# Column norms of the first mixture's weights taken in the middle chunks, and output tiles in another buffer ring, in a fused recurrence and two-mixture kernel

## The chip, the cores and the metric

The kernel runs on one NeuronCore of a Trainium2 chip. The metric is the device time of one execution in microseconds; of several executions the median is quoted. TensorE is called PE here (PEld its weight loads), VectorE DVE, ScalarE ACT, GpSimd POOL, and SyncE SP. The profile gives one execution in detail.

## The reference

Three stages follow each other. A recurrence over 768 time steps (batch 4, 8 heads, width 40), then two feed-forward mixtures over its 3072 x 320 output:

```python
for t in range(S):
    y[:, :, t] = einsum('bhd,bhde->bhe', rt, state)
    Sa = einsum('bhde,bhe->bhd', state, at)
    state = state * wt[:, :, None, :] - einsum('bhd,bhe->bhde', Sa, bt)
    state = state + einsum('bhd,bhe->bhde', vt, kt)
x = y.transpose(0, 2, 1, 3).reshape(B * S, H * D)
h = x @ w_in;   x = (h * cos(h)) @ w_out                          # first mixture, d_ff 2048
h = x @ w_in2;  out = (h * clip(h + 3, 0, 6) / 6) @ w_out2        # second mixture
```

## The kernel before, in words

The recurrence is cut into 12 chunks of 64 steps. A chunk of one batch entry is a unit (48 units), worked through by the functions `pA` to `cF`. The rows `xs` and `x1T` that a chunk leaves are the input of the first mixture for the chunk's 256 tokens, and what the first mixture leaves (`xs2`, transposed by DMA into `x2T` in `mT`) is the input of the second. `mA(m, c, j)` makes one block of the hidden layer of mixture m (m = 0 first, 1 second) for chunk c: 16 matmuls into a PSUM tile `h`, an ACT instruction into a tile `s`, a DVE multiplication in place, and two tiles of `ghl` (a half-precision value and its remainder). `mB(m, c, j)` multiplies such a block with `wout` into the PSUM tiles `acc0` and `acc1` (12 matmuls a block). Eight blocks make a chunk. After the eighth, `mB` copies each `acc` with ACT: for m = 0 into a buffer of the ring `xs2`, for m = 1 into an output tile `ob`, from which `mO` sends two DMAs to `out`.

Buffers are rings (`Rings`): `tile(tag)` hands out the buffers of a tag in turn, in the order in which the functions are called, and a buffer's next writer waits for its last reader. The rings `s` and `xs2` have two buffers each. Before the change `ob` is taken from the ring `s`, so the second `s` tile after it waits until the DMAs of `mO` have read the buffer.

All operations are first recorded by `Plan`, in the order of the numbers given to `at(...)`. That order sets the buffers and the dependences. Then `Plan.order` works out a start for every operation (an estimate of each duration, 50 passes forward and backward over all dependences) and writes the program in that order, engine by engine. So a change of one number in `at` can move rows anywhere in the program. Each engine executes its rows strictly in order, and all DMAs go through SP's queue.

`wcol(q)` (8 calls, line 802) takes the sums of squares of the columns of the first mixture's `win`: three ACT squares into one scratch stretch of `wstat` (called `junk`), two matmuls with a vector of ones after each, into the one PSUM buffer `p` that the units' function `pC` also uses, and a DVE reduction into `acc` (an SBUF table of range values, printed `acc_75` in the order, not the PSUM tiles). Its number is `T_WM + 44 + q`, that is 194 to 201, behind all units. `flags` (line 1164) is recorded last: it folds the table `acc` into one number `bad`. It reduces over the partitions by a DMA of 4 x 128 single elements to DRAM (`std`) and one back into a row, and every engine then loads `bad` and branches: the general version behind the branch is not run with these inputs.

Of the kernel before, what the change touches and what calls it, by code (L numbers as in the profile page):

```python
# [8 lines left out]
F32 = mybir.dt.float32  # L9
# [15 lines left out]
DM = H * D  # L25
# [17 lines left out]
T_P, D_P, T_I, D_I, T_C, D_C, T_M2, T_WM, LAG = 48.0, 2.0, 36.0, 4.0, 29.05, 2.1, 8, 150, 2  # L43
# [456 lines left out]
def kernel(  # L500
# [25 lines left out]
    p2 = Rings(big, 2)  # L526
# [73 lines left out]
    def at(t, fn, *a):  # L600
        heapq.heappush(ev, (t, seq[0], fn, a))
        seq[0] += 1

    def later(dt, fn, *a):
        at(now[0] + dt, fn, *a)
# [8 lines left out]
    def square(src, p0, p1_, n, nm, i, o=None):  # L614
        k = COL[nm][0] + i
        if o is None:
            o = junk[p0:p1_, 0:n]
        if len(src.shape) == 3:
            o = o.rearrange("p (a b) -> p a b", b=src.shape[2])
        nc.scalar.activation(out=o, in_=src, func=AF.Square, accum_out=acc[p0:p1_, k:k + 1])  # L620
# [502 lines left out]
    def mB(m, c, j, h=-1):  # L1123
        gg = G_t.pop((m, c, j, h))
        nf, w = (2, 256) if h < 0 else (4, 128)
        ts = (0, 1) if h < 0 else (h,)
        if j == 0:
            for t in ts:
                ACCS[m, c, t] = ps_a.tile([128, 512], F32, tag=f"acc{t}", name="acc")
        for k in range(nf):  # L1130
            f = nf * j + k
            for n, t in enumerate(ts):
                gs = slice(k * w + n * 128, k * w + (n + 1) * 128)
                for i, (gi, wi) in enumerate(((0, 0), (0, 1), (1, 0))):
                    nc.tensor.matmul(ACCS[m, c, t][:, 0:DM], gg[:, gi, gs], wout[m][:, wi, f, :],
                                     start=(f == 0 and i == 0), stop=(f == 15 and i == 2))
        if nf * (j + 1) < 16:
            return
        for t in ts:
            a = ACCS.pop((m, c, t))[:, 0:DM]  # L1140
            if m == 0:
                xs = p2.tile([128, 768], F16, tag="xs2", name="xs2")
                nc.scalar.activation(out=xs[:, 0:DM], in_=a, func=AF.Copy, scale=ISC)
                nc.vector.scalar_tensor_tensor(out=xs[:, 384:704], in0=a, scalar=ISC, in1=xs[:, 0:DM],
                                               op0=ALU.mult, op1=ALU.subtract)
                xv = xs.rearrange("p (x e) -> p x e", x=2)
                nc.either.tensor_copy(out=xv[:, :, 320:384], in_=xv[:, :, 256:320])
                square(xs[:, 0:DM], 0, 128, DM, "o1", 2 * c + t)
                at(16 * c + 15.8, mT, c, t, xs)
            else:  # L1150
                ob = p2.tile([128, DM], F32, tag="s", name="ob")
                nc.scalar.activation(out=ob, in_=a, func=AF.Copy, scale=ISC2)
                later(0.4, mO, c, t, ob)

# [224 lines left out]
    for c in range(NC):  # L1379
        for m in range(2):  # L1380
            base = 16 * c if m == 0 else 16 * (c + 1) + T_M2 if c < NC - 1 else 16 * NC
            for j in range(8):
                a = (m, c, j) if (m, c) not in HALVES else (m, c, j % 4, j // 4)
                at(base + j + 0.5, mA, *a)
                at(base + j + LAG + 0.9, mB, *a)
# [43 lines left out]
        for i in range(22):  # L1429
            at(T_WM + i + 22 * m, wmax, m, i)  # L1430
    for q in range(8):
        at(T_WM + 44 + q, wcol, q)
    while ev:
        now[0], _, fn, a = heapq.heappop(ev)
        nc.prio, nc.group = now[0], (fn.__name__, now[0]) + tuple(x for x in a if isinstance(x, int))
# [69 lines left out]
```

## Time and profile before

| | |
|---|---|
| median of 3 runs | 1151.99 us (1149.13 to 1154.26) |
| the profiled execution's own time | 1152.2 us |
| its span, first to last instruction | 1149.0 us |
| PE busy | 849.6 us (74%) |
| DVE busy | 987.8 us (86%) |
| ACT busy | 818.9 us (71%) |

The span has three stages. Up to about 350 us weights are loaded and decay products made, and the first chunks begin. From there to about 990 us units and both mixtures are interleaved. After that the mixtures of the last chunks remain, and the range number. A row of the chain view is time on the chain of work that ended last; a row of the timeline gives in brackets how long the engine sat idle and for whom.

### The profile page before, as it was taken

The page shows a single profiled execution, that of the slowest core. Times are in us where ns is not written, and L with a number is a line of the kernel's source. Part 1 is how long each engine was busy: PE and PEld are TensorE (multiplying, and loading weights), DVE is VectorE, ACT ScalarE, POOL GpSimd, SP SyncE. Part 2 cuts the span into 40 slices and gives each one's busy share as a digit, 9 for nine tenths or more (in the row PEclk, how much of TensorE's full clock was granted, in tenths as well). Part 3 has the DMA queues.
Part 4 walks back from the last instruction along what each step waited for, and adds up shares of the span by engine and source line. Part 5 has one row for each costly group of instructions (what it writes and reads, how often), then busy time and mean ns, then how long its engine had stood idle before and what let it go on. Part 6 is the DMA issues. An engine that isn't in the chain of part 4 may idle for free. (4 is left out here: it accounts for less than half of the span.)

```text
span 1149.0 us, 29397 instructions
## 1 busy us (share of the span) xinstructions
PE 849.6 (74%) x11378; PEld 686.3 (60%) x11378; DVE 987.8 (86%) x2359; ACT 818.9 (71%) x1720; POOL 37.6 (3%) x131
## 2 busy tenths in 40 slices
PE   0010123728887989899999788899889989999993
PEld 0000023626675767677877667687667768788872
DVE  7789999999899798798997888988989879998552
ACT  5775578999998797695876867868759756573241
POOL 3000000000000000000000000000000000000000
PEclk9999999957898999999999899899899999999997
DMA  6989878998987878768958768689786744521010
GB/s 213 269 188 274 176 175 167 236 210 180 211 169 148 161 132 141 132 111 166 162 96 167 129 120 160 119 155 149 126 165 122 135 95 74 108 42 34 2 26 16
DMA packets 476279, 162.62 MB, mean 142 GB/s; under 512 B 446405, under 2 KB 458737, under 8 KB 475746
## 3 DMA queue, kind: packets, MB, share of 16 engines
q1 hardware_dynamic: 475842, 159.99, 70.2%
q8 instruction: 91, 1.49, 0.5%
q10 hardware_dynamic: 288, 0.67, 0.2%
q14 instruction: 58, 0.48, 0.1%
HBM read 80.09 MB, written 25.61 MB: 92 GB/s over the span
## 5 line engine op out<-in xcount | busy, mean ns | idle before, releaser
L456 PE MATMUL acc<-wout,ghl 128*128 128x320 f16 x2304 | 362.8, 306 | 24.5 <-DVE ghl L456 17.4
L456 PEld LDWEIGHTS <-win 128*128 128x128 f16 x3328 | 310.8, 101 | 72.3 <-issue 31.4
L456 PEld LDWEIGHTS <-ghl 128*128 128x128 f16 x2304 | 218.6, 100 | 109.8 <-DVE ghl L456 22.8
L456 ACT ACTIVATE s<-h,cvec 128x512 f32<-128x512 f32 x192 | 130.5, 682 | 119.5 <-PE h L456 66.2
L456 PE MATMUL h<-x1T,win 128*128 128x256 f16 (+1 forms) x1664 | 190.4, 272 | 19.8 <-DVE s L456 19.2
L456 PE MATMUL h<-x2T,win 128*128 128x256 f16 (+1 forms) x1664 | 188.2, 269 | 7.1 <-DVE s L456 5.6
L456 DVE TENSOR_TENSOR ghl<-s,ghl 128x512 f16<-128x512 f32 x192 | 130.9, 683 | 5.4 <-ACT ghl L452 3.1
L456 PE MATMUL p<-ART,KBT 120*128 120x64 f16 x384 | 21.9, 206 | 115.6 <-DMA KBT<-KBs 81.0
L456 DVE TENSOR_TENSOR tmp<-Tt,Lt 128x126 f32<-128x126 f32 (+22 forms) x372 | 91.0, 245 | 8.7 <-DMA Lt<-Ls 6.4
L456 DVE SCALAR_TENSOR_TENSOR s<-h,s 128x512 f32<-128x512 f32 x96 | 65.6, 685 | 36.2 <-ACT s L456 35.4
L456 DVE TENSOR_TENSOR Tt<-Tt,tmp 128x126 f32<-128x126 f32 (+22 forms) x372 | 91.0, 245 | 3.1
L456 PEld LDWEIGHTS <-KBT 120*128 120x128 f16 x384 | 18.6, 106 | 119.4 <-DMA KBT<-KBs 102.8
L452 ACT ACTIVATE ghl<-s 128x512 f16<-128x512 f32 x122 | 75.5, 623 | 20.0 <-DVE s L456 17.4
L456 DVE SCALAR_TENSOR_TENSOR s<-s,h 128x512 f32<-128x512 f32 x96 | 64.9, 678 | 20.4 <-ACT s L456 20.2
L456 PE MATMUL t<-E,GF 128*128 128x40 f16 x1152 | 46.0, 184 | 40.4 <-DVE GF L456 37.4
L456 PEld LDWEIGHTS <-GF 128*128 128x128 f16 x1152 | 38.7, 99 | 47.5 <-DVE GF L456 33.5
L452 ACT ACTIVATE Tt<-S8a 40x640 f16<-40x640 f32 (+1 forms) x80 | 47.8, 601 | 7.6 <-DVE S8a L456 4.1
L456 DVE TENSOR_TENSOR Tt<-S8a,Tt 64x320 f16<-64x320 f32 (+1 forms) x92 | 43.7, 483 | 2.8 <-ACT Tt L452 1.7
L456 PEld LDWEIGHTS <-ART 120*128 120x128 f16 (+1 forms) x704 | 43.6, 106 | 4.0 <-issue 1.6
L456 DVE SCALAR_TENSOR_TENSOR wout<-wout 128x512 int32<-128x512 int32 (+1 forms) x56 | 37.9, 680 | 7.9 <-ACT wout L456 7.4
L456 PEld LDWEIGHTS <-TT 128*128 128x128 f16 x768 | 26.6, 98 | 27.2 <-issue 15.7
L456 PE MATMUL q<-Lt 32*32 32x32 f32 x1536 | 22.2, 201 | 27.6 <-DMA Lt<-Tm 20.1
(138 smaller groups left out, 1513.9 us busy)
## 6 DMA issues: line engine op xcount, KB each, us to landing
raw<-in_arbk_dram SPq DMA_DIRECT2D x46, 320.0 KB
v<-in_vv_dram SPq DMA_DIRECT2D x48, 160.0 KB
pip<-Dec SPq DMA_DIRECT2D x46, 160.0 KB
wout<-in_moe_w_in_dram SPq DMA_DIRECT2D x12, 512.0 KB
Ls<-LN SPq DMA_DIRECT2D x48, 128.0 KB
Lt<-Ls SPq DMA_DIRECT2D x48, 128.0 KB
TT<-Thl SPq DMA_DIRECT2D x12, 512.0 KB
wstat<-in_moe_w_out_dram SPq DMA_DIRECT2D x10, 512.0 KB
```

The costliest lines, as they stand in the source:

```text
L452: self.nc.scalar.activation(func=AF.Copy, **kw)
L456: getattr(getattr(self.nc, attr), name)(*a, **kw)
```

## The change

Two lines. The output tiles of all chunks but the first are taken from the ring `xs2`, and `wcol` is recorded at 100.1, 102.1, ... 114.1, among the `pC` of units 36 to 39 and before those of unit 40.

```diff
             else:
-                ob = p2.tile([128, DM], F32, tag="s", name="ob")
+                ob = p2.tile([128, DM], F32, tag="xs2" if c else "s", name="ob")
                 nc.scalar.activation(out=ob, in_=a, func=AF.Copy, scale=ISC2)
                 later(0.4, mO, c, t, ob)
...
     for q in range(8):
-        at(T_WM + 44 + q, wcol, q)
+        at(100.1 + 2 * q, wcol, q)
```

Names in the order carry buffer numbers: `s0_146` and `s1_147` are the two buffers of `s`, `xs20_152` and `xs21_153` those of `xs2`, `acc00_151` and `acc10_154` the PSUM sums, `Tt_93` scratch that `flags` uses, `t0_138` a PSUM tile.

The end of DVE's rows, before: the last multiplication and its two `ghl` rows, then the last norm's reduction, and the range number behind it.

```order
L456 SCALAR_TENSOR_TENSOR s1_147<-s1_147,h1_145 128x512 [waits Activation_49]
L456 CAST ghl2_150<-s1_147 128x512 [waits DVE_49,PE_49]
L456 TENSOR_TENSOR ghl2_150<-s1_147,ghl2_150 128x512 [waits DVE_49,PE_49]
L456 TENSOR_REDUCE acc_75<-p0_134 128x2 [waits PE_49]
L456 TENSOR_SCALAR Tt_93<-acc_75 128x16 [waits DVE_49]
L456 TENSOR_REDUCE Tt_93<-acc_75 128x1
L456 TENSOR_REDUCE Tt_93<-Tt_93 128x1 [waits DVE_49]
L456 TENSOR_REDUCE Tt_93<-Tt_93 1x4 [waits DMAHW4_49]
```

DVE's rows some thirty before the end of the changed program: the last row that `std` needs, three blocks, and the reduction of the row that comes back.

```order
L456 TENSOR_SCALAR Tt_93<-t0_138 72x1 [waits PE_49]
L456 SCALAR_TENSOR_TENSOR s0_146<-s0_146,h0_144 128x512 [waits Activation_49]
L456 CAST ghl1_149<-s0_146 128x512 [waits DVE_49]
L456 TENSOR_TENSOR ghl1_149<-s0_146,ghl1_149 128x512 [waits DVE_49]
L456 SCALAR_TENSOR_TENSOR s1_147<-s1_147,h1_145 128x512 [waits Activation_49]
L456 CAST ghl2_150<-s1_147 128x512 [waits DVE_49]
L456 TENSOR_TENSOR ghl2_150<-s1_147,ghl2_150 128x512 [waits DVE_49]
L456 SCALAR_TENSOR_TENSOR s0_146<-s0_146,h0_144 128x512 [waits Activation_49]
L456 CAST ghl0_148<-s0_146 128x512 [waits DVE_49]
L456 TENSOR_TENSOR ghl0_148<-s0_146,ghl0_148 128x512 [waits DVE_49]
L456 TENSOR_REDUCE Tt_93<-Tt_93 1x4 [waits DMAHW0_49]
L456 SCALAR_TENSOR_TENSOR s1_147<-s1_147,h1_145 128x512 [waits Activation_49]
```

The range number moved from behind the last block to among the last blocks, with four more multiplications after `bad`; the norm's reduction is gone from there.

SP's last rows before the branch, before:

```order
L456 DMA std_156<-Tt_93 128x4x1 [waits DMAHW7_49,DVE_49]
L456 DMA out_0_dram<-s0_146 64x320 [waits DMAHW0_49,Activation_49]
L456 DMA out_0_dram<-s0_146 64x320 [waits DMAHW1_49]
L456 DMA out_0_dram<-s1_147 64x320 [waits DMAHW2_49,Activation_49]
L456 DMA out_0_dram<-s1_147 64x320 [waits DMAHW3_49]
L456 DMA Tt_93<-std_156 1x512 [waits DMAHW7_49,DMAHW4_49]
L1442 TENSOR_LOAD bad_155 [waits DVE_49]
L1444 COMPARE_AND_BRANCH
```

And after the change:

```order
L456 DMA std_156<-Tt_93 128x4x1 [waits DMAHW5_49,DVE_49]
L456 DMA out_0_dram<-xs21_153 64x320 [waits DMAHW6_49,Activation_49]
L456 DMA out_0_dram<-xs21_153 64x320 [waits DMAHW7_49]
L456 DMA Tt_93<-std_156 1x512 [waits DMAHW5_49,DMAHW0_49]
L1442 TENSOR_LOAD bad_155 [waits DVE_49]
L1442 ISA x2
L456 DMA out_0_dram<-xs20_152 64x320 [waits DMAHW1_49,Activation_49]
L456 DMA out_0_dram<-xs20_152 64x320 [waits DMAHW2_49]
L456 DMA out_0_dram<-xs21_153 64x320 [waits DMAHW3_49,Activation_49]
L456 DMA out_0_dram<-xs21_153 64x320 [waits DMAHW4_49]
L1444 COMPARE_AND_BRANCH
```

`std` and the row back now stand a chunk's outputs earlier, and SP loads `bad` ahead of the last four output DMAs.

ACT's rows around the output copies of chunk 9, before (the copies are the two rows from `acc`):

```order
L456 ACTIVATE s0_146<-h0_144,cvec_74 128x512 [waits PE_49,Activation_49]
L456 ACTIVATE s1_147<-h1_145,cvec_74 128x512 [waits DVE_49,PE_49]
L456 ACTIVATE s0_146<-acc00_151 128x320 [waits DVE_49]
L456 ACTIVATE s1_147<-acc10_154 128x320 [waits DVE_49]
L456 ACTIVATE s0_146<-h0_144,cvec_74 128x512 [waits DMAHW5_49,DMAHW6_49,PE_49,Activation_49]
L456 ACTIVATE s1_147<-h1_145,cvec_74 128x512 [waits DMAHW0_49,DMAHW7_49,PE_49,Activation_49]
```

And after the change:

```order
L456 ACTIVATE xs20_152<-acc00_151 128x320 [waits DMAHW2_49,PE_49]
L456 ACTIVATE xs21_153<-acc10_154 128x320 [waits DMAHW4_49,PE_49]
L456 ACTIVATE s0_146<-h0_144,cvec_74 128x512 [waits PE_49]
L452 ACTIVATE ghl0_148<-s0_146 128x512 [waits DVE_49]
L456 ACTIVATE s1_147<-h1_145,cvec_74 128x512 [waits PE_49,Activation_49]
L456 ACTIVATE s0_146<-h0_144,cvec_74 128x512 [waits DVE_49,PE_49]
```

The DMA waits moved from the `s` tiles to the copies themselves; those now wait for the transposes of `xs2` into `x2T`.

## Rows read from the trace of the kernel before

**Rows 1.** Busy time by stretch: us, then PE, PEld, DVE, ACT, POOL, PEclk, DMA.

```profile
350.00:990.00 640.00, 577.53 (x7676) 462.73 (x7674) 566.72 (x1455) 473.51 (x1019) 21.82 (x76) 0.97 0.75 134
990.00:1090.00 100.00, 98.14 (x1124) 81.08 (x1125) 79.35 (x157) 48.74 (x104) 0.00 (x0) 0.98 0.18 37
1090.00:1131.00 41.00, 40.92 (x357) 30.66 (x354) 21.02 (x45) 16.99 (x38) 0.00 (x0) 1.00 0.12 19
1131.00:1149.00 18.00, 0.00 (x0) 0.00 (x0) 1.91 (x7) 0.39 (x1) 0.00 (x0) 0.57 0.14 24
```

**Rows 2.** Waits from 350 to 990 us: us in total, times, longest.

```profile
ACT s L456 <- DMA out_dram<-s: 22.7, 12, 4.2
DVE s L456 <- ACT s L456: 28.3, 25, 3.3
PE h L456 <- DVE s L456: 15.0, 19, 2.2
```

**Rows 3.** Timeline of ACT, two `s` tiles behind outputs: start, us, instruction, idle before.

```profile
919.20 0.69 ACT L456 ACTIVATE s<-h,cvec 128x512 f32<-128x512 f32 x1 [3.53 <-DMA out_dram<-s]
924.34 0.69 ACT L456 ACTIVATE s<-h,cvec 128x512 f32<-128x512 f32 x1 [4.19 <-DMA out_dram<-s]
```

**Rows 4.** Busy time in the eleven stretches around such waits, first, last, sum.

```profile
456.30:461.50 5.20, 4.11 (x34) 2.73 (x31) 2.15 (x5) 0.69 (x1) 0.00 (x0) 1.00 0.48 112
...
920.10:926.40 6.30, 3.42 (x86) 2.71 (x86) 2.61 (x5) 2.07 (x6) 0.00 (x0) 1.00 0.95 155
sum 43.70, PE 33.45 PEld 25.08 DVE 25.96 ACT 15.58 POOL 0.00; mean PE 3.04 PEld 2.28 DVE 2.36 ACT 1.42 POOL 0.00
```

**Rows 5.** The chain of waits at 990 us, and PE's wait there.

```profile
989.49 2.15 DMA out_dram<-s
...
PE q L456 <- ACT Lt L456: 1.6, 1, 1.6
```

**Rows 6.** The chain while PE is full, one block of each kind.

```profile
1057.33 1.75 PE h L456 x16
1059.08 1.63 PE acc L456 x12
```

**Rows 7.** Groups of instructions from 1090 to 1131 us.

```profile
L456 ACT ACTIVATE wstat<-win 128x256 bf16<-128x256 f16 (+1 forms) x23 | 9.5, 411 | 7.4 <-PE p L456 7.4
L456 DVE SCALAR_TENSOR_TENSOR s<-s,h 128x512 f32<-128x512 f32 x10 | 6.8, 684 | 11.3 <-ACT s L456 11.3
L456 PE MATMUL p<-cvec,wstat 128*128 128x1 bf16 (+1 forms) x48 | 4.7, 166 | 0.0
L456 DVE TENSOR_REDUCE acc<-p 128x2 f32<-128x6 f32 x8 | 1.3, 158 | 3.5 <-PE p L456 3.5
```

**Rows 8.** The chain where the norms' matmuls stand in it.

```profile
1092.56 0.03 PE p L456 x2
...
1094.69 0.13 PE p L456 x2
...
1096.18 0.84 PE acc L456 x6
...
1098.02 0.92 PE acc L456 x6
```

**Rows 9.** Timeline of the end.

```profile
1128.87 0.42 SPq L456 DMA_DIRECT2D std<-Tt  x1
...
1130.61 2.40 SPq L456 DMA_DIRECT2D out_dram<-s  x4
1130.96 0.44 ACT L456 ACTIVATE s<-acc 128x320 f32<-128x320 f32 x1 [0.38 <-PE acc L456]
...
1140.67 1.27 DVE L456 TENSOR_REDUCE Tt<-Tt 1x4 f32<-1x512 f32 x2 [11.83 <-DMA Tt<-std]
...
1142.57 0.14 DVE L456 TENSOR_SCALAR bad<-Tt 1x1 int32<-1x1 f32 x1
```

**Rows 10.** Timeline of PE: unit 39's product into `p`, and its first use.

```profile
773.99 0.40 PE L456 MATMUL p<-ART,KBT 120*128 120x64 f16 x8
...
878.50 0.20 PE L456 MATMUL t<-FS,NT 128*128 128x40 f16 x2
```

## The prediction

> **What bounds the kernel now.** I read the busy time by stretch first, then the chain of waits from its end, then the waits of ACT, DVE and PE in the middle, and the timeline of the last 25 us.
>
> From 990 us until the last block PE has no gap to speak of: 98.14 of 100 us and 40.92 of 41 us are busy [rows 1], and the chain runs on PE, 1.75 us for a block of `h` and 1.63 us for a block of `acc` [rows 6]. So when attention is done, PE still has some 140 us of mixture work in hand, and PE's last block comes when PE has worked off everything. What counts in the middle is PE's idle time there: 640 less 577.5, or 62.5 us, and DVE, on which PE mostly waits, is idle for 73.3 us of the same stretch [rows 1].
>
> The end is different. PE's last sum is done at 1130.96, where ACT starts the last copy [rows 9]; the span ends 18.0 us later, at 1149.0. In that tail PE does nothing. DVE's last norm reduction and the range number stand behind the last block; then `std` and the row back take 11.83 us before DVE can go on, `bad` is written at 1142.71, and 6.3 us more pass to the span's end [rows 9]. The outputs are issued by 1133.01, so they don't set the end.
>
> **The change, part by part.**
>
> *The range number leaves the end.* The norms were its last input. In the changed order `std` is issued seven `h` blocks before the end, `bad` is written four blocks before it, and SP has loaded `bad` before it issues the last outputs; its branch has no wait of its own. What is left behind PE's last sum is the copy and the issue of four DMAs, 1133.01 - 1130.96 = 2.05 us [rows 9], and the closing stretch of 6.3 us: 8.4 us instead of 18.0, a gain of **9.6 us**. Bounds: if the outputs must land (2.15 us for such a DMA, rows 5) before the closing stretch can begin, 10.5 us stay and the gain is 7.5; if the closing stretch lies wholly beside the landing, 4.2 stay and the gain is 13.8. I take 9.6, since the order shows no wait at the branch, yet nothing that would shorten the closing stretch. The 6.3 us come after a branch. The Trainium skill ("Runtime: NRT & Kernel Launch", Instruction fetch mechanics) says that a taken branch whose target isn't in the window forces a DMA fetch of the target page before execution can go on. No row here shows what fills those 6.3 us; by that rule they stay, which is what I took without it.
>
> *A new wait takes its place.* DVE now meets the row that comes back from `std` among the last blocks, and the multiplication of the next block is queued behind it. `std` leaves once PE's small matmul of the range number is done. From there PE has four `h` blocks and three `acc` blocks, 4 x 1.75 + 3 x 1.63 = 11.9 us [rows 6], until it needs the `h` buffer that the delayed multiplication frees. DVE gets there after 11.83 us of DMA and half of the two reductions' 1.27 us [rows 9], and 0.68 us of multiplication [rows 7]: 13.1 us. PE stands still for 1.2 us and the hand-overs; I take **1.5 us** lost, between 0 and the 13.1 us itself if none of the cover holds. PE waits for that multiplication, ACT's next `s` too.
>
> *The norms' own work.* 24 ACT squares (0.41 us), 48 matmuls and 8 DVE reductions (0.16 us) [rows 7] leave a stretch in which only PE is full. On the chain their matmuls cost 0.03 us for each of 16 pairs and 0.13 for each of 8 half-high ones, and the six `acc` matmuls behind the latter take 0.92 instead of 0.84 [rows 8]: 0.5 + 1.0 + 0.6 = 2.2 us of PE. In the middle PE spends the same 2.2 us again. ACT's 10.0 us are hidden there, since ACT is idle for 166 of 640 us [rows 1]; if that cover failed they would show as late `s` tiles. DVE's 1.3 us may show. The net is between -2.2 us (the middle has room) and +1.3 us; I take **0**, because what PE owes it pays in either place. The norms also hold `p`, so `pC` of unit 40 stands later: 1399 PE rows behind that of unit 39 where it was 492. Units have a lead for that: unit 39's product is made at 774.0 us and first used at 878.5 [rows 10], 104 us later. In the changed order unit 40's product still stands 1627 rows ahead of its use (2257 before), so no unit is made late.
>
> *Output copies leave the ring `s`.* In the middle ACT waits 22.7 us, in 12 waits, for output DMAs to read an `s` buffer [rows 2], up to 4.19 us at a time [rows 3]; DVE then waits for `s` and PE for DVE [rows 2]. One of the twelve, 1.4 us, is chunk 0's and stays. Around the other eleven there are 43.70 us in which PE is busy for 33.45 and DVE for 25.96 [rows 4]. At the middle's mean idle shares (9.8% and 11.5%, rows 1) they would be idle for 4.3 and 5.0 us; they are idle for 10.25 and 17.7. The excess is 6.0 us of PE and 12.7 us of DVE. One more such wait stands on the chain at 990 us, and PE is idle for 1.6 us there [rows 5]. PE's own loss is **7.6 us**, and I take it as the gain, since PE's backlog sets the end. Bounds: 0, if PE meets other waits in the same places; 12.7 + 1.6 = 14.3, if all that DVE gets back arrives. The copies have a new wait instead, for the transposes into `x2T` that read `xs2`. In the changed order both transposes stand ahead of the outputs in SP's queue, and more than 850 PE matmuls lie between a chunk's last `h` and its last sum in every chunk of the middle, so I cost it at nothing.
>
> *The sum.* -9.6 + 1.5 + 0 - 7.6 = -15.7 us. The profiled execution took 1152.2 us (span 1149.0 and 3.2 around it), which is the median of the runs within 0.2. Forecast: 1136.5 us, its own bounds from all terms at their good end (-13.8 - 2.2 - 14.3 = -30.3, 1122) to all at their bad end short of the lost cover (-7.5 + 3 + 1.3 = -3.2, 1149); I call it the forecast between 1129 and 1145.
>
> **The rivals.**
>
> *DVE is the limit of the middle.* Then the vector time that comes back counts in full: 14.3 instead of 7.6, and the norms' 2.2 us leave PE's end: 1136.5 - 6.7 - 2.2 = 1127.6, and down to 1123 with a shorter closing stretch. For it: PE's weight loads fill only 462.7 of 640 us there while DVE fills 566.7 [rows 1]. Against it: the last 140 us are PE's alone. The Trainium skill ("Perfetto Trace Analysis", Identifying the Most-Contended Engine) says that matmul busy time is no good measure and that weight-load busy time should be used; by that, 72% for PE against 89% for DVE, DVE is the engine to relieve in the middle. The trace agrees for the middle and not for the last 140 us, where PE is back to back.
>
> *The middle gives nothing.* The whole program is planned anew, and what PE waited for can come back in other places: outputs 0, norms +1.3, the new wait 3, the tail -7.5 to -9.6. That is -3 to -5.5, 1147 to 1149. For it: the rows differ from the very first chunk on, not only around the edit. Against it: the eleven waits have no other cause, and their buffers are free now.
>
> *Slower: the flag's way through DRAM holds up the last blocks.* Place: DVE's reduction among the last blocks, with PE's end behind it. Today the 11.83 us cost PE nothing, because PE is done. `std` is 512 single elements, and it now shares SP's queue with outputs and the mixture's DMAs. Beyond the 11.9 us of cover each further microsecond is PE's. At 35 us in all PE loses 23 us more and the run takes 1160; it is slower by 0.5% from 33 us on. Against it: the DMA engines are busy for 0.12 of the last stretch [rows 1], and today's `std` shares its time with four outputs too.
>
> *It doesn't do what it says.* The range number could still end last, if `bad` came after the last outputs: the row back at 13 us and `bad` some 2 us later against more than 25 us of PE work after `std` speak against it. Then only the middle gains: about 1144.
>
> **How the numbers follow.** A measurement of this kernel tells 0.5%, 5.8 us, from no change: faster is below 1146.2, slower above 1157.8. Forecast 0.62, DVE the limit 0.13, the middle gives nothing 0.18, slower 0.04, not as it says 0.03. Faster: 0.62 + 0.13 + 0.03 and a third of the third case, 0.06: 0.84. Same: 0.12. Slower: 0.04. The range takes in the forecast, most of the DVE case and half of the third: 1125 to 1147.
>
> **What would show it.** The tail: from PE's last sum to the span's end 8 to 9 us, with `bad` written before the last copies. The new wait: DVE idle for the row from `std` for 2 to 3 us among the last blocks, PE for 1 to 2 us behind it. The outputs: no wait of ACT for output DMAs outside chunk 0, and PE's idle time from 350 us to its last block down by 7 us from 64. The norms: squares and their matmuls amid units, none in the last 130 us. It is wrong if PE's idle time in the middle is the same or more, if PE waits for `t`, `acc` or `h` in new places, or if the last blocks stand still for the flag.

## The result, and the profile after

The changed kernel takes 1134.1 us (median; 1133.61 to 1135.95), the kernel before beside it 1150.6: a ratio of 0.9862, with a 95% interval from 0.9823 to 0.9900. That is 11.5 to 20.4 us less; 15.7 were forecast. The profiled execution took 1134.04 us, its span is 1132.2.

Busy time by stretch in the changed kernel, columns as in [rows 1]; the last boundary is ACT's last copy, which starts when PE's last sum is done:

```profile
350.00:990.00 640.00, 586.32 (x7911) 472.66 (x7911) 579.12 (x1484) 489.91 (x1060) 21.81 (x76) 0.96 0.72 137
990.00:1090.00 100.00, 97.89 (x1007) 80.04 (x1005) 78.23 (x158) 46.05 (x100) 0.00 (x0) 0.98 0.14 28
1090.00:1125.35 35.35, 34.12 (x277) 26.75 (x275) 18.28 (x36) 7.78 (x13) 0.00 (x0) 1.00 0.08 16
1125.35:1132.20 6.85, 0.00 (x0) 0.00 (x0) 0.00 (x0) 0.44 (x1) 0.00 (x0) 0.87 0.23 56
```

The last row is the tail: 6.85 us where it was 18.0. PE's last sum itself comes 5.6 us earlier, at 1125.35 instead of 1130.96 [rows 9]. PE is busy for the same 849.8 us up to there (849.6 before), so what went is idle time: 8.8 us less from 350 to 990 us (53.7 instead of 62.5), 2.1 more from 200 to 350 us, 1.2 more in the last row but one, the rest small.

The end of the changed kernel, as in [rows 9] (start, us, instruction, idle before and for whom):

```profile
1108.78 0.26 SPq L456 DMA_DIRECT2D Tt<-std  x1
1110.45 0.67 DVE L456 TENSOR_REDUCE Tt<-Tt 1x4 f32<-1x512 f32 x1 [5.58 <-DMA Tt<-std]
1111.77 1.91 PE L456 MATMUL h<-x2T,win 128*128 128x256 f16 x16 [1.19 <-DVE s L456]
1113.38 0.14 DVE L456 TENSOR_SCALAR bad<-Tt 1x1 int32<-1x1 f32 x1
1125.00 2.39 SPq L456 DMA_DIRECT2D out_dram<-xs  x4
1125.35 0.44 ACT L456 ACTIVATE xs<-acc 128x320 f32<-128x320 f32 x1 [0.38 <-PE acc L456]
```

`bad` is written 12 us ahead of the last copy. DVE waits 5.58 us for the row from `std`, and the `h` block behind it stands still for 1.19 us. The outputs are issued by 1127.39, and the span ends 4.8 us later.

Waits from 350 to 990 us, as in [rows 2]:

```profile
DVE s L456 <- ACT s L456: 17.7, 27, 2.2
PE p L456 <- DVE LN L456: 11.5, 5, 4.0
PE t L456 <- DVE TT L456: 10.2, 13, 2.0
PE h L456 <- DVE s L456: 6.6, 7, 2.5
PE acc L456 <- ACT Tt L452: 4.3, 1, 4.3
```

PE's wait for `s` has fallen from 15.0 to 6.6 us, ACT's 22.7 us for output DMAs have shrunk to 0.8, and other waits of PE have grown. These are three of them in the kernel before:

```profile
PE acc L456 <- DVE ghl L456: 9.9, 8, 2.6
PE t L456 <- DMA FT<-FS: 4.4, 4, 1.9
PE p L456 <- DVE LN L456: 1.0, 2, 0.6
```

The wait of `p` for `LN` has risen from 1.0 to 11.5 us, and PE now waits 4.3 us for ACT's `Tt` ahead of an `acc`, which it did not before. The norms' matmuls stand from 726.8 to 816.2 us. Most of that looks as forecast. The experiments show that one part of it isn't what it looks like.

### The profile page after: what moved, and what is told of

Read it like the earlier page. It is cut to its first block, busy times and chain, and to the rows that moved or that the text cites. A ratio compares the mean times of both kernels' runs of the same rounds, so it can differ in the third digit from the quotient of the medians.

```text
span 1132.2 us, 29403 instructions
## 1 busy us (share of the span) xinstructions
PE 849.8 (75%) x11378; PEld 688.1 (61%) x11378; DVE 989.6 (87%) x2357; ACT 817.4 (72%) x1722; POOL 37.6 (3%) x131
## 5 line engine op out<-in xcount | busy, mean ns | idle before, releaser
L456 PEld LDWEIGHTS <-ghl 128*128 128x128 f16 x2304 | 219.8, 100 | 100.1 <-DVE ghl L456 13.9
L452 ACT ACTIVATE ghl<-s 128x512 f16<-128x512 f32 x129 | 80.5, 625 | 28.5 <-DVE s L456 24.5
L456 DVE SCALAR_TENSOR_TENSOR s<-s,h 128x512 f32<-128x512 f32 x96 | 65.1, 678 | 11.2 <-ACT s L456 10.9
L456 PE MATMUL t<-FS,NT 128*128 128x40 f16 x768 | 37.8, 184 | 22.3 <-DVE uls L456 9.9
L456 PEld LDWEIGHTS <-ART 120*64 120x64 f16 (+1 forms) x704 | 44.0, 106 | 8.9 <-issue 6.4
L456 DVE SCALAR_TENSOR_TENSOR wout<-wout 128x512 int32<-128x512 int32 (+1 forms) x56 | 37.9, 683 | 10.3 <-ACT wout L456 10.2
L456 PEld LDWEIGHTS <-NT 128*128 128x128 f16 x768 | 32.8, 99 | 21.7 <-DVE uls L456 10.1
```

The source lines that it names most:

```text
L452: self.nc.scalar.activation(func=AF.Copy, **kw)
L456: getattr(getattr(self.nc, attr), name)(*a, **kw)
```

## The experiments

Ratios are to the kernel before, run beside each on the same chip, with 95% intervals. "Own order" means that the rows stand on every engine just as in the kernel named; without that, `Plan.order` has worked the program out anew.

### The output tiles alone, in the old order, and planned anew

`own_frozen` gives the output tiles other buffers after the order is fixed:

```diff
                 nc.scalar.activation(out=ob, in_=a, func=AF.Copy, scale=ISC2)
+                if c:
+                    OB2[c, t] = wstat[:, 320 * t:320 * t + DM]
+                    nc.ops[-1]["calls"][-1][3]["out"] = OB2[c, t]
```

(and the same for the source of the output DMAs). `out_only` is the first line of the change without the second. `own_end` lets the plan know of the buffers in `wstat`: `ob = wstat[:, 320 * t:320 * t + DM] if c else ...`, with the norms still at the end.

> The kernel before, row for row in its own order on every engine; only the buffers of the output tiles of chunks 1 to 11 are others: two stretches of the scratch wstat that nobody uses after the weights are converted (351 us), instead of the ring s. So this is the buffers' part alone, without a new plan and without a new wait for the transposes. My theory (what PE lost at the output waits comes back): ACT's waits for out_dram go from 22.7 us to about 1, PE's idle time from 350 to 990 us falls from 62.5 to about 56, the wait at 990 us goes too, and the time falls by 7.6 us: 1144.5, ratio 0.993. If DVE were the limit of the middle: 14.3 us, 1138, ratio 0.988. If PE only meets other waits in the same places, and after's gain in the middle came from the new plan: PE's idle time stays at 61 to 63 us, ratio 0.998 to 1.001. The tail behind PE's last sum stays at 18.0 us.

> The kernel before with the output tiles in the ring xs2 (planned anew), the norms still behind the last unit. My theory: tail 18.0 us as before, PE's idle time from 350 to 990 us about 55, time 1144 (ratio 0.993), and the new wait for x2T's transposes costs nothing. If a new plan by itself moves PE's idle time by several us, it can differ from own_frozen by as much, either way; if the transposes cost something, ACT waits for x2T and the ratio is 0.996 or more.

> The norms stay behind the last unit as before, the output tiles of chunks 1 to 11 get unused scratch of their own, and the program is planned anew with that (the run own_frozen had the same buffers in the old order, 0.999; out_only had the ring xs2 and a new plan, 0.998). Theory A (a ring that ties the plan less gives better plans, whatever the end looks like; out_only had an unlucky one): PE's idle time from 350 to 990 us 54 to 58 instead of 62.5, ratio 0.990 to 0.995. Theory B (freer output tiles give something only with the norms in the middle): ratio 0.996 to 1.002. The tail behind PE's last sum is 18 us in both.

Measured: `own_frozen` 0.9992 (0.9969 to 1.0015), `out_only` 0.9976 (0.9951 to 1.0001), `own_end` 0.9884 (0.9854 to 0.9914). Busy time in `own_frozen` from 350 to 990 us and in two of the stretches of [rows 4], then its waits from 350 to 990 us:

```profile
350.00:990.00 640.00, 579.03 (x7697) 463.63 (x7693) 568.83 (x1460) 475.41 (x1023) 22.07 (x76) 0.97 0.77 134
...
456.30:461.50 5.20, 4.49 (x89) 3.10 (x88) 2.13 (x4) 0.34 (x1) 0.00 (x0) 1.00 0.55 130
920.10:926.40 6.30, 4.23 (x98) 3.14 (x97) 1.64 (x4) 2.26 (x6) 0.00 (x0) 1.00 0.96 191
```

```profile
DVE s L456 <- ACT s L456: 16.5, 22, 1.8
PE acc L456 <- DVE ghl L456: 12.1, 10, 2.5
PE h L456 <- DVE s L456: 10.4, 15, 1.5
PE t L456 <- DMA FT<-FS: 6.3, 4, 2.2
```

ACT's wait for output DMAs is gone from the list altogether, DVE's wait for ACT has fallen from 28.3 to 16.5 us, and in the two stretches PE is busy for 0.38 and 0.81 us more than before [rows 4]. So the mechanism is there. But PE's idle time in the middle is 61.0 us where it was 62.5: what is won beside an output is given back at other waits. PE waits 4.6 us less for `s`, 2.2 more for `ghl`, 1.9 more for `FT`. The forecast of this run, 0.993, fell; the third theory in its expectation held. `out_only`, for which 0.993 was expected too, shows no gain clear of noise either.

`own_end` has the same buffers, the same norms at the end, and another order. Its middle and its tail:

```profile
350.00:990.00 640.00, 585.91 (x7926) 474.08 (x7924) 578.05 (x1466) 486.13 (x1045) 22.53 (x76) 0.97 0.74 136
1119.23:1137.20 17.97, 0.00 (x0) 0.00 (x0) 1.91 (x7) 0.44 (x1) 0.00 (x0) 0.62 0.10 24
```

PE's idle time in the middle is 54.1 us, as in the changed kernel, and the tail is still 18.0. So freer buffers with a new plan give some 13 us here, more than either theory expected, though the bare removal of the waits gives nothing. Not all of the 13 us is idle time. PE's last sum comes 11.7 us earlier than in the kernel before (1119.23 against 1130.96): PE is idle for 4.6 us less up to there, and the same matmuls keep it busy for 7.1 us less (842.6 instead of 849.6), with a granted clock of 0.86 instead of 0.83 from 200 to 350 us and of 1.00 instead of 0.97 from 990 to 1050. `out_only` shows that freed buffers don't have to help: its plan brought no gain that this measurement can tell. Why that plan is no better than the old one stays open.

### The norms alone, in two places and with freed buffers

`norms_only` is the second line of the change without the first. `norms_own_frozen` is the same in its own order, with the output tiles in `wstat` as in `own_frozen`. `norms_only_92` records the norms at other numbers:

```diff
-        at(100.1 + 2 * q, wcol, q)
+        at(92.1 + 2 * q, wcol, q)
```

> The changed kernel with the output tiles back in the ring s: the norms in the middle alone (planned anew). My theory: the tail behind PE's last sum 7 us instead of 18.0 (11 us gained), DVE waits for the row from std among the last blocks and PE 1.2 us behind it, the norms' own work costs nothing net, ACT still waits some 22 us for out_dram in the middle and PE's idle time there stays near 62: 1142, ratio 0.991. If after's gain in the middle had nothing to do with the output tiles: PE's idle time near 54 and 1134, ratio 0.986. If the end's gain is lost elsewhere: 1149 to 1152.

> The run with the norms moved alone (output tiles in s, 0.994), row for row in its own order, with the output tiles of chunks 1 to 11 in unused scratch: no wait of ACT for out_dram is left, and no engine's order changes. Theory A (the ring ties the plan, not the chip: a wait taken away in a fixed order only uncovers the next one, and the gain comes when the rows are set in another order): no change from that run, 0.992 to 0.996, PE's idle time from 350 to 990 us 57 to 59 (58.9 there). Theory B (with the norms in the middle the output waits do cost PE time while the chip runs): most of what separates it from the changed kernel comes back, 0.985 to 0.989, PE idle 50 to 54.

> Output tiles in the ring s as before, norms in the middle at 92.1 to 106.1 instead of 100.1 to 114.1: a second plan with the ring s. If the ring holds back every plan by some 10 us: 0.990 to 0.997, about as the first (0.994). If the changed kernel merely had the luckier plan: it can as well be as fast as the changed kernel, 0.983 to 0.989.

Measured: 0.9943 (0.9917 to 0.9969), 0.9936 (0.9909 to 0.9962) and 0.9874 (0.9843 to 0.9906). For `norms_only` 0.991 was expected. The tails are 6.7, 7.1 and 6.6 us. Again freed buffers in a fixed order change nothing that the timed runs can tell (theory A), and a second plan with the ring `s` is 0.007 faster than the first, as its second theory allowed.

At the end of `norms_only` the two edits turn out to meet. Its last blocks, and the DMA on the chain there:

```profile
1106.33 9.68 DMA out_dram<-s
1116.11 1.27 ACT L456 ACTIVATE s<-h,cvec 128x512 f32<-128x512 f32 x2 [9.14 <-DMA out_dram<-s]
1117.58 3.57 PE L456 MATMUL h<-x2T,win 128*128 128x256 f16 x16 [4.13 <-DVE s L456]
```

An output DMA that is issued behind `std` takes 9.68 us here, where one took 2.15 in [rows 5]. ACT waits 9.14 us for it to read its `s` buffer, PE then stands still for 4.13 us, and its next `h` block takes 3.57 us instead of 1.91. It is the same in `norms_only_92` (9.21, 4.19 and 3.54 us). The changed kernel has none of this, because its output tiles are not in `s`. `norms_own_frozen` has no such wait of ACT either; 2.4 us of PE's wait are left there, behind the row from `std`.

ACT's wait for outputs and the busy time from 350 to 990 us in `norms_only_92`, then the busy time in `norms_own_frozen`:

```profile
ACT s L456 <- DMA out_dram<-s: 31.0, 11, 5.5
```

```profile
350.00:990.00 640.00, 584.65 (x7923) 472.92 (x7923) 568.97 (x1465) 492.85 (x1070) 21.10 (x76) 0.97 0.71 136
```

```profile
350.00:990.00 640.00, 580.10 (x7726) 465.19 (x7724) 567.82 (x1466) 487.14 (x1053) 21.96 (x76) 0.96 0.74 135
```

The middle alone would mislead here. The first kernel waits for output DMAs longer than the one before the change, 31.0 us, and PE is idle for 55.4 us. In the second only chunk 0's wait of 3.1 us is left, and PE is idle for 59.9. Counted from the start to 1050 us, the two are alike (280.5 and 280.6 us idle), and what separates their last sums, 1128.18 and 1134.08, is PE's busy time, 843.4 and 850.8 us.

### The same two edits with the norms elsewhere

`norms_84`, `norms_92` and `norms_116` are the changed kernel with 84.1, 92.1 or 116.1 instead of 100.1.

> Output tiles in the ring xs2, norms at 84.1 to 98.1: a fourth plan with that ring. If the ring makes the difference, 0.980 to 0.987 again, with PE's idle time from 350 to 990 us 50 to 55 and a tail of 7 us; if plans differ by luck, 0.989 or more.

> Output tiles in the ring xs2 as in the changed kernel, norms at 92.1 to 106.1: a third plan with that ring (the other two gave 0.986 and 0.981). If the ring makes the difference: 0.980 to 0.987, that is under the run with the ring s at the same place by 0.008 or so. If plans differ by luck: it can be 0.989 or more.

> The changed kernel with the norms recorded one chunk later (116.1 to 130.1 instead of 100.1 to 114.1): a new plan, and nothing else that should matter. My theory: PE's idle time from 350 to 990 us 52 to 56 as in the changed kernel (53.7), tail about 7, time 1132 to 1137 (ratio 0.983 to 0.988). If what the middle gained was the luck of one plan: PE's idle time differs by over 4 us from 53.7 and the time with it, 1138 or more, or 1130 or less.

Measured:

| norms at | output tiles in `s` | in `xs2` | in unused scratch |
|---|---|---|---|
| the end | 1 (the kernel before) | 0.9976 | 0.9884 |
| 100.1 | 0.9943 | 0.9862 (the change) | |
| 92.1 | 0.9874 | 0.9794 | |
| 84.1 | | 0.9746 | |
| 116.1 | | 0.9813 | |

In a row, planned anew, freed output tiles give 0.008 twice, 0.012 once and nothing that can be told once. In a column, a number that should not matter moves the ratio by as much: 0.0116 from 100.1 to 84.1. 0.9746, 0.9794 and 0.9813 are all below what the first theory of each had expected. The tail is 6.6 to 7.2 us in all six kernels of this table with the norms in the middle and 17.9 to 18.0 in the three with the norms at the end.

Here is PE's time up to its last sum, from one profiled execution of each kernel:

| kernel | idle up to 1050 us | idle behind that | busy |
|---|---|---|---|
| before | 281.3 | 0.0 | 849.6 |
| `own_frozen` | 280.2 | 0.0 | 850.0 |
| `norms_only` | 281.1 | 4.2 | 847.6 |
| `norms_own_frozen` | 280.6 | 2.6 | 850.8 |
| `norms_only_92` | 280.5 | 4.2 | 843.4 |
| `out_only` | 282.4 | 0.0 | 850.2 |
| `own_end` | 276.6 | 0.0 | 842.6 |
| the change (100.1) | 274.3 | 1.2 | 849.8 |
| `norms_92` | 275.1 | 1.5 | 843.7 |
| `norms_84` | 274.1 | 1.4 | 841.0 |
| `norms_116` | 274.0 | 1.6 | 849.5 |

The idle time is 1050 us less PE's busy time in lines like these, of the kernel before, `own_frozen` and the changed kernel:

```profile
0.00:1050.00 1050.00, 768.72 (x10685) 622.43 (x10686) 942.05 (x2267) 789.51 (x1659) 37.55 (x131) 0.96 0.77 153
0.00:1050.00 1050.00, 769.82 (x10692) 622.37 (x10693) 942.38 (x2268) 788.53 (x1660) 37.82 (x131) 0.96 0.78 153
0.00:1050.00 1050.00, 775.71 (x10769) 628.62 (x10770) 949.68 (x2283) 798.55 (x1688) 37.56 (x131) 0.95 0.75 154
```

Two executions with the same rows up to there differ by up to 2.7 us (`norms_84_late`, below, 271.4; `std_3`, below, 276.6). Beyond that the table falls into two groups. With the output tiles in `s`, or freed in an order that was planned for `s`, PE is idle for 280.2 to 281.3 us. With the tiles freed and the program planned anew it is idle for 274.0 to 276.6 us, wherever the norms stand; `out_only` alone falls out. So the neutral number does not move PE's idle time. What differs among those four traces is PE's busy time, 841.0 to 849.8 us. (The profiled execution of `norms_116`, 1134.07 us, is its slowest; its median is 1130.34.)

Where does 84.1 beat 100.1? Busy time of `norms_84` and then of the changed kernel from 200 to 350 us, and each one's sums up to PE's last sum:

```profile
200.00:350.00 150.00, 105.06 (x1629) 87.77 (x1618) 141.25 (x316) 141.93 (x300) 3.17 (x11) 0.86 0.90 200
...
sum 1116.47, PE 840.97 PEld 683.25 DVE 987.98 ACT 818.17 POOL 39.23; mean PE 168.19 PEld 136.65 DVE 197.60 ACT 163.63 POOL 7.85
```

```profile
200.00:350.00 150.00, 103.45 (x1512) 84.85 (x1510) 141.16 (x314) 138.67 (x292) 3.16 (x11) 0.82 0.94 197
...
sum 1125.35, PE 849.83 PEld 688.13 DVE 989.60 ACT 816.95 POOL 37.56; mean PE 169.97 PEld 137.63 DVE 197.92 ACT 163.39 POOL 7.51
```

PE's idle time up to its last sum is the same, 1116.47 - 840.97 = 275.5 and 1125.35 - 849.83 = 275.5 us. The whole 8.9 us are busy time: the same matmuls at a higher granted clock, 0.86 instead of 0.82 early on and 0.98 instead of 0.96 in the middle. Why one order is granted more clock than another was not tested. Between the changed kernel and the one before there is no such difference (849.8 and 849.6 us busy).

### The wait for the row from `std`

`std_3` sends `std` three times, in the changed kernel's own order (`nc.std` is that row's number, noted in `flags`):

```diff
         for i in self.order():
             self.emit(i)
+            if i == self.std:
+                self.emit(i)
+                self.emit(i)
```

> The changed kernel in its own order, with the DMA of 512 single elements (std) sent three times, one behind the other, so that the row comes back some 19.6 us later (9.8 us for one in the changed kernel). My theory (DVE waits for the row with the next multiplication behind it, and PE's cover is used up: it stands still for 1.2 us as it is): PE stands still for about 20.8 us among the last blocks and the time is 1153 to 1154, ratio 0.999 to 1.003. If PE had cover left, or the wait were off the path: under 1140, ratio under 0.990.

Measured: 1.0055 (1.0033 to 1.0078). PE's block behind the wait, and busy time around it:

```profile
1130.77 3.57 PE L456 MATMUL h<-x2T,win 128*128 128x256 f16 x16 [20.40 <-DVE s L456]
```

```profile
1110.00:1130.77 20.77, 0.37 (x4) 0.13 (x3) 1.32 (x4) 0.02 (x1) 0.00 (x0) 0.63 0.05 8
1130.77:1137.00 6.23, 6.23 (x31) 4.23 (x31) 5.20 (x13) 1.87 (x3) 0.00 (x0) 0.57 0.02 5
```

PE stands still for 20.40 us instead of 1.19, 19.2 more, as DVE's wait for the row grows by 19.2 (from 5.58 to 24.79). So no cover was left, and the wait is on the path, microsecond for microsecond. What was not expected is the second window: behind the stop PE is granted 0.57 of its clock, the block takes 3.57 us instead of 1.91, and PE's last sum comes 21.6 us later, 2.4 more than the stop. The median, 1158.9 against 1134.1, is later by more than that and lies above the 1153 to 1154 that were expected; the mean granted clock of these runs is 0.939 to 0.950 and that of the changed kernel's 0.951 to 0.960, but what sets it was not tested.

`norms_84_late` takes the wait from PE's path instead. On the kernel `norms_84`, DVE's seven rows that need the row back go behind the block (1, 11, 4):

```diff
-        for i in self.order():
+        od = self.order()
+        n = len(od) - 7
+        od = [i for i in od if i < n]
+        p = max(k for k, i in enumerate(od) if self.ops[i]["grp"][0][0] == "mA" and self.ops[i]["grp"][0][2:] == (1, 11, 4))
+        for i in od[:p + 1] + list(range(n, n + 7)) + od[p + 1:]:
```

> The run with the norms at 84.1 (0.975), with DVE's seven rows of the range number that need the row back from std moved two blocks later; no other row moves. My theory (the multiplication is no longer queued behind the wait): PE's 1.4 us among the last blocks go and the time falls by 1.2 to 1.5 us, 1123, ratio 0.9735, DVE's idle time for the row falls from 5.8 to 0, and the tail of 7.2 us stays, since bad is still written some 8 us before PE's last sum. If that wait was off the path, or bad's later time lengthens the tail: no change, 0.975.

Measured: 0.9730 (0.9700 to 0.9760), 1122.9 us, against 0.9746 (0.9720 to 0.9773) for `norms_84`. In the traces, `norms_84` first, then this one:

```profile
1101.57 0.67 DVE L456 TENSOR_REDUCE Tt<-Tt 1x4 f32<-1x512 f32 x1 [5.78 <-DMA Tt<-std]
1102.89 1.91 PE L456 MATMUL h<-x2T,win 128*128 128x256 f16 x16 [1.39 <-DVE s L456]
1116.47 0.44 ACT L456 ACTIVATE xs<-acc 128x320 f32<-128x320 f32 x1 [0.38 <-PE acc L456]
```

```profile
1102.56 1.26 DVE L456 TENSOR_REDUCE Tt<-Tt 1x4 f32<-1x512 f32 x2
1104.46 0.14 DVE L456 TENSOR_SCALAR bad<-Tt 1x1 int32<-1x1 f32 x1
1115.07 0.44 ACT L456 ACTIVATE xs<-acc 128x320 f32<-128x320 f32 x1 [0.38 <-PE acc L456]
```

Both waits are gone, and `bad` is written no later than before. PE's last sum is 1.4 us earlier, and the tail stays at 7.2. From DVE's last row ahead of `std`, which starts at 1089.64 and at 1089.78, to the last sum it is 25.29 us instead of 26.83. That is below what the timed runs can tell apart, so it rests on the trace. The median is the lowest of the study, but its interval overlaps that of `norms_84`.

### The norms' own price

`no_norms` emits nothing of `wcol`, in the changed kernel's own order:

```diff
         for i in self.order():
-            self.emit(i)
+            if self.ops[i]["grp"][0][0] != "wcol":
+                self.emit(i)
```

> The changed kernel in its own order, without the norms: the 24 squares, 48 matmuls and 8 reductions are left out (the columns' bound is then not tested), all other rows stand as they were. My theory (PE pays its 2.2 us in the middle as it did at the end, ACT's and DVE's parts are hidden): 1131 to 1133, ratio 0.981 to 0.984, PE's last sum 1 to 3 us earlier. If the middle hides them all: as the changed kernel, 0.986. If their squares hold up ACT or the buffer p holds up the units: 5 us or more, under 1129.

Measured: 0.9878 (0.9852 to 0.9903), beside 0.9862 (0.9823 to 0.9900) with the norms: no gain. From 350 to 990 us:

```profile
350.00:990.00 640.00, 585.27 (x7851) 471.70 (x7850) 578.10 (x1476) 482.47 (x1035) 22.24 (x76) 0.96 0.72 137
```

ACT is busy for 7.4 us less, and PE's idle time is 54.7 instead of 53.7 us. Up to its last sum, which comes 0.8 us earlier, PE is busy for 2.2 us less (847.6 instead of 849.8) and idle for 1.4 us more; two executions of the same rows can differ by as much. In the middle the norms cost nothing that the timed runs can tell; the second theory of the expectation held. PE's wait of `p` for `LN` is 11.1 us without the norms and 11.5 with them, so it is not the norms' use of `p` that makes it.

## Why the prediction was right, and where it was not

**The range number leaves the end: right, a little too small.** 9.6 us were forecast, 11.2 came, within the bounds of 7.5 and 13.8. The term that was off is the closing stretch: 6.3 us were carried over, but with `bad` written long before only 4.8 us follow the last output's issue. `own_end`, where `bad` is last again, has 6.2 us behind it. The prediction had noted that SP now loads `bad` ahead of the last outputs; whether that load is the difference was not tested. In the changed kernel and both 84.1 kernels 4.6 to 4.9 us follow the last output's issue. The Trainium skill ("Runtime: NRT & Kernel Launch", Instruction fetch mechanics) says that a taken branch whose target is out of the fetched window waits for a DMA fetch. That would leave a stretch at the end wherever `bad` is written, and these figures agree with it, though the last output's landing lies in them too and no run shows what fills them.

**The new wait: right.** 1.5 us were taken, 1.19 came, by the way that was worked out: DVE's reduction with the next multiplication queued behind it. `std_3` shows the rival's price line (each further microsecond is PE's), and `norms_84_late` that the order alone decides it. DVE's own wait for the row was forecast at 2 to 3 us and is 5.58; the sum did not use it. What the prediction left out is that the outputs behind `std` are held up as well, and that this is where its two edits meet: with the norms moved and the tiles left in `s`, as in `norms_only`, PE waits 4.13 us among the last blocks and runs the next one at 0.52 of its clock.

**The norms' own work: right.** 0 was taken and `no_norms` shows 0 to within its interval. The squares and matmuls stand amid units, as forecast.

**Output copies leave the ring `s`: the size right, the step to it wrong.** The failed step is "PE's own loss is 7.6 us, and I take it as the gain, since PE's backlog sets the end". In a fixed order the loss doesn't come back: PE's idle time up to 1050 us goes from 281.3 to 280.2 us in `own_frozen` and from 281.1 to 280.6 in `norms_own_frozen`, the lower bound of that term, 0, "if PE meets other waits in the same places". The idle time of engines that wait for each other in strict order can't be summed up around one kind of wait and called that wait's price. PE's idle time ahead of the last blocks did fall in the changed kernel, by 7.0 us (281.3 to 274.3 up to 1090 us), and by 6.2 to 7.3 us up to 1050 us in all four plans with both edits. So it takes the freed buffers and the new plan together; neither the freed buffers in the old order nor a new plan with the ring `s` did it, and `out_only` had both without it. How the new order saves PE those waits was not shown, nor whether the nearness of 7.0 to 7.6 is more than luck. The prediction's own signs of being wrong came in part: PE waits longer for `t` behind `TT` (10.2 us instead of 6.6) and in a new place for `acc`.

The term that was missing from the range is PE's busy time, which the sum took as the same before and after. It is, in the changed kernel (849.8 and 849.6 us). With the norms at 84.1 or 116.1 the same edits gave 0.9746 and 0.9813, and the range's low end, 1125, would just not have held the former (1124.5): its PE is busy for 841.0 us.

**The new wait for the transposes: right.** No wait of ACT's copies for `x2T` stands in the changed kernel's list.

**The rivals.** DVE as the limit of the middle would have given 1127.6: `own_frozen` removes ACT's waits and much of DVE's behind them, and the kernel gets no faster (0.9992). "The middle gives nothing" was right for each fixed order, and wrong for the program as planned. The flag's way through DRAM did not hold up the last blocks beyond 1.19 us; `std_3` puts its point of decision where it was said to lie.

## What to carry to other kernels

Work that only feeds a final decision belongs ahead of the last blocks: most of the latency behind the last sum goes (11.2 of 18.0 us here), and the price is one wait in the queue of an engine, which a few rows' order removes. A wait that is seen in the trace is a price only if nothing else ends just after it; to learn that, take the wait away with every row in its place. Two edits that each look separate can meet in a queue: here the one moves a slow DMA ahead of the transfers that the other's buffers wait for. And where a planner sets the order, an edit is two edits, its own and the new plan: time a few neutral numbers beside it, and part PE's time into idle and busy, before its gain is put down to a mechanism.

## What the hardware showed beside that

- PE's granted clock differs between plans and between runs of one plan, and it is worth as much as the edits. 12 runs of `norms_only` lie between 1136.8 us, at a mean of 0.963, and 1150.8, at 0.950; two kernels with the same idle time, the changed one and `norms_84`, differ by 8.9 us of busy time.
- After 20.4 us without work PE is granted 0.57 of its clock over the next 6.2 us, and an `h` block takes 3.57 us instead of 1.91; while that block runs, the granted clock is 0.50, the lower of its two levels (1.2 of 2.4 GHz). After 4.13 us without work in `norms_only` the block takes 3.57 us too, at 0.52; after 1.19 us in the changed kernel it takes 1.91, at 1.00.
- Output DMAs that are issued behind `std`, a DMA of 512 single elements, land late: 9.68 and 9.71 us on the chains of `norms_only` and `norms_only_92`, against 2.15 [rows 5].
- Three DMAs of 512 single elements, one behind the other, take 9.22, 8.57 and 9.64 us on the chain of `std_3`, each nearly as long as the one in the changed kernel (9.81):

```profile
1098.69 9.22 DMA std<-Tt
1107.93 8.57 DMA std<-Tt
1116.52 9.64 DMA std<-Tt
```
